# A third PSUM bank for attention, taken from the first products, with a new listed order

## The chip, the cores and the metric

The kernel runs on one core of a Trainium2 chip. Its engines work side by side: TensorE (PE) multiplies matrices and writes into PSUM, which has eight banks of 128 partitions x 512 float32 here; VectorE (DVE) and ScalarE (ACT) read PSUM, compute and write SBUF; GpSimd (POOL) issues a few transfers; the queue of SyncE (SP) issues nearly all loads and stores. The metric is the device time of one execution in microseconds (us).

## The reference

A linear attention with a decaying state is followed by two feed-forward layers with 3072 tokens, 384 features and 2048 hidden features.

```python
# attention: 4 x 8 heads, 768 steps, 48 features
state = alpha[:, :, t, :, None] * state + einsum('bhd,bhe->bhde', k[:, :, t], v[:, :, t])
y[:, :, t] = einsum('bhd,bhde->bhe', q[:, :, t], state)
...
# layer 0
h = x @ w_in                       # 3072 x 384 by 384 x 2048
g = where(h >= 1, h, where(h <= -1, 0, (h + 1) ** 2 / 4))
x = g @ w_out                      # 3072 x 2048 by 2048 x 384
...
# layer 1, with its own weights
h = x @ w_in
g = h * clip(h + 3, 0, 6) / 6
out = g @ w_out
```

## The kernel before

**Attention** is cut into 24 units: 12 groups of 256 tokens, each with two halves of the heads. The groups' pieces of 64 tokens are done as matrix products. A unit u goes through these steps, named here by the words that the kernel's list uses: loads by SP's queue (`L`, `Lp`, `Lk`, `Lq`, `V`); running products and scalings on VectorE (`p`, `r`, `s`, `k`, `R`; L380 to L409); transposition of the keys `T` (TensorE, L425) and its copy `kt` (ScalarE, L430); scores `S` (TensorE, L442) and their mask `m` (VectorE, L452); states of the pieces `ST` (TensorE, L468), their sums `h` (VectorE, L480 and L484) and copies `st` (ScalarE, L491); outputs `O` (TensorE, L515), copied out by `xc` (ScalarE, L541) and `xl` (VectorE, L546). Each of `T`, `S`, `ST` and `O` takes one PSUM bank of the pool `ps_a` (`ps_att`), in turn, and the bank is free when the engine behind it (`kt`, `m`, `h`, `xc` or `xl`) has read it.

**The layers** work on blocks of 512 tokens, six a layer, and on 16 steps of 128 hidden features a block. A step f has a first product `A` of nine matmuls of 128x512 into a bank of the pool `ps_h` (`ph`, L121), a gate, and a second product `B` of nine matmuls (L162) that add up in the three banks of `ps_o`. In layer 0 the gate is three steps of ScalarE (L141, L142, L143) and one of VectorE (L151), which frees the bank `ph`; then ScalarE (L154) and VectorE (L791) split the result in a high and a low part for `B`. In layer 1 the gate is one step of ScalarE (L146) and L153, L154, L791. The eight first steps of block 0 (phase 0) take plain float32 operands instead (L129 for `A`, L135 for `B`, six passes each). An `A` takes the next bank of `ps_h`, so with three banks the `A` of step f waits for the gate of step f - 3.

**Weights** come in 768 KB tiles, one a step (`LW`, L305), and are converted before use: L79 (ScalarE, `ca`), L85, L90, L96 (VectorE, `cb`, `cc`, `cd`), then a high part L113 (ScalarE) and a low part L114 (VectorE); in the list the high and low parts are `hi` (L708) and `lo` (L712). Layer 0's weights are converted in the first 100 us or so, layer 1's while the last block of layer 0 and the first of layer 1 run, from 480 us; their loads go through a ring of two buffers (`qkv_sb`). The input of a block of layer 1 is split by L168 (ScalarE) and L169 (VectorE).

**What sets the order.** From the start into the third phase the string `ORDER` (L39 to L64) gives the order: a word is a step with its unit or weight number (`A0_4` is the first product of phase 0, step 4), and `in_order` ties each instruction to the one before it on its engine. `Wn` (L339) are n filler matmuls into a bank of `ps_h` that compute nothing and keep TensorE busy while it would wait. Phases that follow are written as a loop, and the framework sets each engine's order there from the dependences and from when tiles of its pools come free; the numbers of banks go into that order.

Of the kernel before, what the change touches and what calls it, by code (L numbers as in the profile page):

```python
# [44 lines left out]
g0_1 V6 mx0_0 LW6 p8 B0_0 ca7 mx0_1 g0_2 r8 LW10 cb3 cc3 B0_1 ca6 mx0_2 LW9 cd3 hi2 k5 hi3 A0_3 z3 R5 gd3
LW8 cc4 Rc5 cd4 ca9 B0_2 Lp7 Lk7 cc5 g0_3 cd5 R6 Lq7 T5 ca8 mx0_3 S5 kt5 r6 p7 Rc6 A0_4 ca10 R7 r7 Rc7 s7
ST5 g0_4 k7 A0_5 h5 mx0_4 gd5 m5 st5 B0_3 s6 g0_5 s8 S7 k8 O5 m7 B0_4 V7 xc5 R8 L9 xl5 Rc8 k6 mv4 cb7 T6 cc7
S6 kt6 cd7 ST6 m6 A0_7 h6 cb6 st6 cc6 T7 cd6 O6 kt7 z6 lo3 gd6 ST7 V8 lo1 xc6 LW14 A0_6 h7 hi7 xl6 st7 lo7
LW13 hi5 O7 z7 mx0_5 gd7 p9 T8 V9 B0_5 xc7 R9 LW11 kt8 xl7 g0_6 lo2 mv6 ST8 lo5 LW12 g0_7 mx0_6 S8 h8 B0_6
m8 st8 Rc9 z8 mx0_7 gd8 lo0 O8 hi6 r9 B0_7 s9 L10 hi4 ca13 k9 ca11 lo4 A1_0 oc0 lo6 V10 cb9 LW15 cb10 A1_1  # L50
g1_0 cc10 p10 A1_2 g1_1 mx1_0 cb8 cb15 A1_3 gh1_0 mx1_1 ca15 gl1_0 cc15 g1_2 A1_4 cd15 cc8 gh1_1 T9 ca12
mx1_2 B1_0 gl1_1 kt9 gh1_2 cd8 g1_3 B1_1 gl1_2 cb12 cc12 g1_4 A1_5 mx1_3 cc9 hi8 mx1_4 A1_6 gh1_4 lo8 gh1_3
gl1_4 ca14 B1_2 gl1_3 g1_6 cd9 B1_3 r10 s10 hi9 g1_5 mx1_6 B1_4 k10 lo9 gh1_6 A1_7 mx1_5 xc8 gl1_6 gh1_5
cd10 A1_8 gl1_5 hi10 xl8 g1_7 lo10 S9 cb13 ST9 g1_8 m9 B1_5 h9 mx1_7 st9 cd12 A1_10 gh1_7 z9 gl1_7 gd9 mx1_8
# [842 lines left out]
```

## Time and profile before

| | us |
|---|---|
| median of 3 runs | 934.08 (934.04 to 934.58) |
| the profiled execution | 933.03 |
| its span in the trace | 931.1 |
| TensorE busy | 912.6 (98%) |
| VectorE busy | 530.9 (57%) |
| ScalarE busy | 531.2 (57%) |
| granted TensorE clock, mean | 0.996 |

The span runs from the first to the last instruction of the trace. Busy times are totals; filler matmuls count as busy. The views used below are the timeline (one row for a run of like instructions: its start, its length, what it writes and reads, and in brackets the idle time of its engine before it with the event that ended it), the list of waits, the table by stretch, and the groups of instructions by line. In a timeline row "issue" as a releaser means that the profile shows no wait.

### The profile page before, as it was taken

What the parts mean: (1) busy time and instruction counts of PE and PEld (TensorE: products, weight loads), DVE (VectorE), ACT (ScalarE), POOL (GpSimd) and SP (SyncE); (2) the same over time, 40 slices, a digit from 0 to 9 for tenths busy, and PEclk for the clock granted to TensorE, in tenths of its full rate; (3) what the DMA queues carried; (4) which work ended last, traced back from release to release, by engine and by line L of the source; (5) the groups of instructions that cost most, each with busy time, mean ns of one, the idle gap of its engine ahead of it and who ended that gap; (6) DMA issues with size and microseconds to landing.
All of it is one profiled execution on the core that took longest, in us unless ns stands there. A gap on an engine that the chain in (4) does not pass through costs nothing.

```text
span 931.1 us, 14299 instructions
## 1 busy us (share of the span) xinstructions
PE 912.6 (98%) x5800; PEld 726.3 (78%) x5805; DVE 530.9 (57%) x856; ACT 531.2 (57%) x855; POOL 40.3 (4%) x88
## 2 busy tenths in 40 slices
PE   7899999999999999999999999999999999999996
PEld 4646688888887888888888788888888888888885
DVE  8889989745665656565448985333433433333332
ACT  3786986785667666776777864433433433333332
POOL 1201101010100100000000000000000000000000
PEclk9999999999999999999999999999999999999999
DMA  8983602121223222221024430000000000000001
GB/s 313 331 306 109 231 2 77 63 73 40 98 72 125 83 72 72 69 86 57 6 69 137 135 136 1 34 1 0 34 1 1 34 0 1 34 1 1 34 1 38
DMA packets 18892, 69.34 MB, mean 74 GB/s; under 512 B 3457, under 2 KB 3777, under 8 KB 16513
## 3 DMA queue, kind: packets, MB, share of 16 engines
q1 hardware_dynamic: 16224, 66.07, 20.3%
q0 software_dynamic: 2304, 2.17, 1.1%
q8 instruction: 48, 0.79, 0.4%
q14 instruction: 28, 0.22, 0.1%
q10 hardware_dynamic: 288, 0.10, 0.1%
HBM read 61.44 MB, written 4.72 MB: 71 GB/s over the span
## 4 chain that ended last, share of the span: by engine, by line
PE 89%; DMA 5%; DVE 4%; ACT 1%; issue 1%; SPq 0%; DVEq 0%; ACTq 0%
PE po L162 39%; PE ph L121 38%; PE ps_att L515 2%; PE ps_att L468 2%; DMA qkv_sb<-in_wgt 2%; PE ps_att L442 2%; PE po L135 2%; PE ph L129 2%; DMA x<-in_wgt 1%; DMA qkv_sb<-in_qkv 1%; PE ps_att L425 1%; DVE w L114 0%; DVE qkv_sb L90 0%; DVE qkv_sb L380 0%; DVE qkv_sb L394 0%
## 5 line engine op out<-in xcount | busy, mean ns | idle before, releaser
L162 PE MATMUL po<-g,w 128*128 128x512 f32 x1656 | 410.9, 392 | 0.0
L121 PE MATMUL ph<-x,w 128*128 128x512 f32 x1512 | 370.6, 390 | 0.4 <-DVE t L151 0.4
L162 PEld LDWEIGHTS po<-g,w 128*128 128x128 f32 x1656 | 308.2, 188 | 64.8
L121 PEld LDWEIGHTS ph<-x,w 128*128 128x128 f32 x1512 | 282.9, 188 | 60.7 <-DVE t L151 1.2
L791 DVE TENSOR_TENSOR g<-t,g 128x512 fp32r<-128x512 f32 x160 | 110.5, 690 | 101.8 <-ACT g L154 101.6
L154 ACT ACTIVATE g<-t 128x512 fp32r<-128x512 f32 x160 | 100.9, 632 | 107.5 <-DVE t L153 63.2
L153 DVE SCALAR_TENSOR_TENSOR t<-t,ph 128x512 f32<-128x512 f32 x96 | 66.0, 688 | 157.5 <-ACT t L146 157.5
L146 ACT ACTIVATE t<-ph,half 128x512 f32<-128x512 f32 x96 | 66.0, 688 | 156.8 <-PE ph L121 155.1
L141 ACT ACTIVATE t<-ph,half 128x512 f32<-128x512 f32 x96 | 65.6, 684 | 38.6 <-PE ph L121 35.7
L151 DVE TENSOR_TENSOR t<-t,ph 128x512 f32<-128x512 f32 x64 | 43.6, 681 | 44.3 <-ACT t L143 44.0
L143 ACT ACTIVATE t<-t 128x512 f32<-128x512 f32 x96 | 60.7, 632 | 2.7
L142 ACT ACTIVATE t<-t 128x512 f32<-128x512 f32 x96 | 60.6, 631 | 2.4
L121 PE MATMUL ph<-turns,w 128*128 128x512 f32 x144 | 36.9, 396 | 0.0
L556 POOL DMA_DIRECT2D x<-stage x48 | 24.4, 514 | 263.8 <-DVE x L546 77.5
L380 DVE TENSOR_TENSOR_SCAN qkv_sb<-qkv_sb,zero 128x256 f32<-128x256 f32 x40 | 25.4, 676 | 12.1 <-DMA qkv_sb<-in_qkv 12.1
L121 PEld LDWEIGHTS ph<-turns,w 128*128 128x128 f32 x144 | 26.8, 188 | 6.1
L452 DVE TENSOR_TENSOR R<-ps_att,mask 64x512 int32<-64x512 int32 x40 | 27.5, 689 | 5.2 <-PE ps_att L442 4.5
L491 ACT ACTIVATE st<-sh 64x384 f32<-64x384 f32 x48 | 25.0, 521 | 9.6 <-DVE sh L484 8.4
L394 DVE TENSOR_TENSOR_SCAN qkv_sb<-qkv_sb,recs,zero 128x256 f32<-128x256 f32 x40 | 27.8, 737 | 0.6
L515 PEld LDWEIGHTS ps_att<-R,st 128*64 128x64 f32 x640 | 20.8, 138 | 9.2 <-issue 4.2
L468 PEld LDWEIGHTS ps_att<-qkv_sb,kt 64*64 64x64 f32 (+1 forms) x576 | 20.2, 135 | 7.7 <-issue 3.2
L515 PE MATMUL ps_att<-R,st 128*64 128x64 f32 x640 | 23.6, 225 | 2.4 <-DVE sh L480 1.8
(108 smaller groups left out, 656.7 us busy)
## 6 DMA issues: line engine op xcount, KB each, us to landing
qkv_sb<-in_qkv SPq DMA_DIRECT2D x18, 1216.0 KB, 5.5
qkv_sb<-in_wgt SPq DMA_DIRECT2D x16, 768.0 KB, 4.2
w<-in_wgt SPq DMA_DIRECT2D x10, 768.0 KB, 7.1
st<-in_vst SPq DMA_DIRECT2D x48, 128.0 KB, 3.1
x<-in_wgt SPq DMA_DIRECT2D x4, 768.0 KB, 12.2
out<-x SPq DMA_DIRECT2D x12, 256.0 KB, 2.2
w<-in_qkv SPq DMA_DIRECT2D x4, 512.0 KB, 7.9
w<-in_qkv SPq DMA_DIRECT2D x4, 448.0 KB, 5.3
```

The costliest lines, as they stand in the source:

```text
L121: nc.tensor.matmul(ph, w[:, a, 0, j * P:(j + 1) * P], x[:, b, j], start=(i == 0), stop=(i == 3 * KD - 1))
L141: nc.scalar.activation(t, ph, AF.Relu, scale=-0.5, bias=half)
L142: nc.scalar.activation(t, t, AF.Relu, scale=-1.0, bias=1.0)
L143: nc.scalar.activation(t, t, AF.Square)
L146: nc.scalar.activation(t, ph, AF.Relu, scale=1.0 / 6.0, bias=half)
L151: nc.vector.tensor_tensor(out=t, in0=t, in1=ph, op=ALU.max)
L153: nc.vector.scalar_tensor_tensor(out=t, in0=t, scalar=1.0, in1=ph, op0=ALU.min, op1=ALU.mult)
L154: nc.scalar.activation(g[:, 0], t, AF.Copy)
L162: nc.tensor.matmul(po[m], w[:, a, 1, m * P:(m + 1) * P], g[:, b], start=(first and i == 0), stop=(last and i == 2))
L468: nc.tensor.matmul(ps[C * h:C * h + C, c, r, :], n["kt"][k0:P, 2 * r + 1 - c // 2, C * h:C * h + C], n["v"][k0:P, 1 - c // 2, 2 * r + h, : ...
L515: nc.tensor.matmul(ps[C * h:C * h + C, r, cs], s[:, h, r, c, :], R[:, h, r, cs], start=True, stop=True)
L791: nc.vector.tensor_tensor(out=g[:, 1], in0=tt, in1=g[:, 0].bitcast(F32), op=ALU.subtract)
```

## The change

The pool of attention banks gets three instead of two, the pool of first products two instead of three. The string `ORDER` is written anew for that: the same steps in another order, and fillers of 38 matmuls in eight words instead of 35 in eight (beside the 24 before it).

```diff
-    ps_a = ctx.enter_context(tc.tile_pool(name="ps_a", bufs=2, space=PSUM))
-    ps_h = ctx.enter_context(tc.tile_pool(name="ps_h", bufs=3, space=PSUM))
+    ps_a = ctx.enter_context(tc.tile_pool(name="ps_a", bufs=3, space=PSUM))
+    ps_h = ctx.enter_context(tc.tile_pool(name="ps_h", bufs=2, space=PSUM))
...
-T1 W6 kt1 R2 V1 h0 Rc2 V0 r2 S1 LW1 s2 ST1 m1 st0 W1 LW2 h1 O0 k2 st1 p3 T2 V2 xc0 LW0 kt2 R3 O1 r3 ca2 s3
...
+Lp2 Lk2 m0 T1 S1 kt1 z0 p3 gd0 O0 Lq3 m1 ST1 xc0 V2 p2 W13 LW0 r2 h1 LW1 s2 st1 O1 k2 ca0 r3 LW3 T2 s3 xc1
```

What moves at three places follows, before and after, without the fillers where "..." stands.

On TensorE, at the start of the attention. L425 is a transposition, L442 scores, L468 states, L515 outputs; `ps_att_...` is the bank's tile, `st0` and `st1` are the states of units 0 and 1. Before:

```order
L425 MATMUL ps_att_159<-cst_sb_89,qkv_sb_137 128x128 x4
L442 MATMUL ps_att_173<-R_157,qkv_sb_137 64x64 x16
L468 MATMUL ps_att_192<-qkv_sb_137,kt_171 64x48 x16
...
L425 MATMUL ps_att_225<-cst_sb_89,qkv_sb_140 128x128 x4
...
L442 MATMUL ps_att_252<-R_190,qkv_sb_140 64x64 x16
L468 MATMUL ps_att_273<-qkv_sb_140,kt_237 64x48 x16
...
L339 MATMUL ph_294<-filler_90 128x512
L515 MATMUL ps_att_302<-R_157,st0_127 64x64 x16
L425 MATMUL ps_att_324<-cst_sb_89,w15_144 128x128 x4
L515 MATMUL ps_att_340<-R_190,st1_128 64x64 x16
```

After:

```order
L425 MATMUL ps_att_157<-cst_sb_89,qkv_sb_137 128x128 x4
...
L468 MATMUL ps_att_176<-qkv_sb_137,kt_167 64x48 x16
L442 MATMUL ps_att_200<-R_173,qkv_sb_137 64x64 x16
...
L425 MATMUL ps_att_233<-cst_sb_89,qkv_sb_140 128x128 x4
L442 MATMUL ps_att_238<-R_162,qkv_sb_140 64x64 x16
L515 MATMUL ps_att_261<-R_173,st0_127 64x64 x16
L468 MATMUL ps_att_281<-qkv_sb_140,kt_255 64x48 x16
...
L339 MATMUL ph_305<-filler_90 128x512
...
L515 MATMUL ps_att_333<-R_162,st1_128 64x64 x16
L425 MATMUL ps_att_356<-cst_sb_89,w15_154 128x128 x4
```

The outputs of unit 0 now stand right behind the scores of unit 1 and ahead of its states; the states of unit 0 stand ahead of its scores.

On TensorE, in the last block of layer 0, where layer 1's weights are converted (from about 508 us in the trace). `w12` is the weight of step 12, `ph_...` the bank's tile of its first product, `po0` the first bank of the second products, each of which has nine rows of which the first stands here. Before:

```order
L121 MATMUL ph_4842<-x_3756,w12_1620 128x512 x9
L162 MATMUL po0_4530<-g_4767,w9_1363 128x512
...
L121 MATMUL ph_4878<-x_3756,w13_1647 128x512 x9
L162 MATMUL po0_4530<-g_4794,w10_1413 128x512
...
L121 MATMUL ph_4905<-x_3756,w14_1669 128x512 x9
L162 MATMUL po0_4530<-g_4830,w11_1588 128x512
...
L121 MATMUL ph_4941<-x_3756,w15_1721 128x512 x9
L162 MATMUL po0_4530<-g_4866,w12_1620 128x512
```

After:

```order
L121 MATMUL ph_4845<-x_3759,w12_1504 128x512 x9
L162 MATMUL po0_4533<-g_4797,w10_1308 128x512
...
L121 MATMUL ph_4881<-x_3759,w13_1547 128x512 x9
L162 MATMUL po0_4533<-g_4833,w11_1326 128x512
...
L121 MATMUL ph_4908<-x_3759,w14_1579 128x512 x9
L162 MATMUL po0_4533<-g_4869,w12_1504 128x512
...
L121 MATMUL ph_4944<-x_3759,w15_1654 128x512 x9
L162 MATMUL po0_4533<-g_4896,w13_1547 128x512
```

Each first product now has the second product of a step one later ahead of it: that of step 14 stands behind the second product of step 11 instead of step 10.

On ScalarE, at the end of the same block. `t_4924` and `t_4927` belong to the gate of step 14, `t_4960` and `t_4963` to step 15, `g_4929` and `g_4932` are the high part of step 14's result. Before:

```order
L142 ACTIVATE t_4924<-t_4924 128x512
L143 ACTIVATE t_4924<-t_4924 128x512
L168 ACTIVATE x_5266<-x1_94 128x1536
L113 ACTIVATE w9_5022<-qkv_sb_4922 128x768
L141 ACTIVATE t_4960<-ph_4941,half_92 128x512
L154 ACTIVATE g_4929<-t_4924 128x512
L79 ACTIVATE qkv_sb_4958<-qkv_sb_4958 128x768
```

After:

```order
L142 ACTIVATE t_4927<-t_4927 128x512
L113 ACTIVATE w9_5025<-qkv_sb_4925 128x768
L154 ACTIVATE g_4896<-t_4891 128x512
L143 ACTIVATE t_4927<-t_4927 128x512
L79 ACTIVATE qkv_sb_4961<-qkv_sb_4961 128x768
L141 ACTIVATE t_4963<-ph_4944,half_92 128x512
L168 ACTIVATE x_5269<-x1_94 128x1536
L154 ACTIVATE g_4932<-t_4927 128x512
```

The split L168, which stood right behind step 14's gate, now stands behind a conversion (L79) and the first gate step of step 15; the high part of step 14 stands behind it as before.

Elsewhere in the loop's phases first and second products alternate in both kernels.

## Rows read from the trace of the kernel before

**Rows 1.** Page, part 1: engine, busy us (share of the span), instructions
```profile
PE 912.6 (98%) x5800; PEld 726.3 (78%) x5805; DVE 530.9 (57%) x856; ACT 531.2 (57%) x855; POOL 40.3 (4%) x88
```

**Rows 2.** List of waits of TensorE, 60 to 925 us: total, times, longest (us)
```profile
PE ph L129 <- DVE w L96: 1.3, 1, 1.3
PE ph L121 <- DVE t L151: 0.4, 1, 0.4
```

**Rows 3.** Table by stretch: length, busy us by engine, PEclk, DMA share, GB/s
```profile
10.00:60.00 50.00, 42.09 (x551) 27.69 (x554) 43.93 (x85) 34.49 (x57) 6.51 (x13) 0.97 0.97 338
30.00:40.00 10.00, 8.81 (x142) 6.99 (x143) 9.53 (x18) 7.20 (x15) 2.52 (x6) 0.83 0.90 317
480.00:560.00 80.00, 79.61 (x350) 65.27 (x349) 68.11 (x94) 61.96 (x93) 0.00 (x0) 1.00 0.41 138
```

**Rows 4.** Timeline of TensorE, 8 to 31 us: start, length, ..., idle before
```profile
14.55 0.63 PE L425 MATMUL ps_att<-cst_sb,qkv_sb 128*128 128x128 f32 x4 [0.52 <-issue]
15.02 1.46 PE L339 MATMUL ph<-filler 128*128 128x512 bf16 x6
...
20.38 1.24 PE L515 MATMUL ps_att<-R,st 128*64 128x64 f32 x32 [1.77 <-DVE sh L480]
...
22.71 1.31 PE L515 MATMUL ps_att<-R,st 128*64 128x64 f32 x32 [0.50 <-issue]
...
30.72 0.49 PE L468 MATMUL ps_att<-w,kt 64*64 64x48 f32 x10 [2.21 <-ACT kt L430]
```

**Rows 5.** Timeline of VectorE, 12 to 36 us
```profile
18.74 1.39 DVE L452 TENSOR_TENSOR R<-ps_att,mask 64x512 int32<-64x512 int32 x2
...
29.23 1.39 DVE L452 TENSOR_TENSOR w<-ps_att,mask 64x512 int32<-64x512 int32 x2
```

**Rows 6.** Timeline of TensorE, 30 to 70 us
```profile
33.39 3.28 PE L515 MATMUL ps_att<-w,st 128*64 128x64 f32 x64
...
45.59 8.19 PE L129 MATMUL ph<-xf,w 128*128 128x512 f32 x18
...
67.18 2.85 PE L129 MATMUL ph<-xf,w 128*128 128x512 f32 x6
```

**Rows 7.** Timeline of ScalarE, 40 to 58 us
```profile
45.14 0.94 ACT L79 ACTIVATE w<-w 128x768 f32<-128x768 f32 x1 [1.85 <-DMA w<-in_wgt]
...
55.82 0.96 ACT L79 ACTIVATE x<-x 128x768 f32<-128x768 f32 x1 [1.51 <-DMA x<-in_wgt]
```

**Rows 8.** Timeline of TensorE near 292 us
```profile
292.81 2.25 PE L121 MATMUL ph<-turns,w 128*128 128x512 f32 x9
```

**Rows 9.** Timeline of VectorE near 292 us
```profile
291.92 0.68 DVE L151 TENSOR_TENSOR t<-t,ph 128x512 f32<-128x512 f32 x1
```

**Rows 10.** Timeline of TensorE, 500 to 530 us
```profile
516.81 2.20 PE L121 MATMUL ph<-x,w 128*128 128x512 f32 x9
518.85 2.20 PE L162 MATMUL po<-g,w 128*128 128x512 f32 x9
521.44 2.34 PE L121 MATMUL ph<-x,w 128*128 128x512 f32 x9 [0.40 <-DVE t L151]
```

**Rows 11.** Timeline of VectorE, 505 to 532 us
```profile
520.71 0.68 DVE L151 TENSOR_TENSOR t<-t,ph 128x512 f32<-128x512 f32 x1
...
527.92 1.76 DVE L169 TENSOR_TENSOR x<-x,x 128x1536 fp32r<-128x1536 f32 x1 [0.19 <-ACT x L168]
```

**Rows 12.** Timeline of ScalarE, 505 to 532 us
```profile
526.41 1.48 ACT L168 ACTIVATE x<-x 128x1536 fp32r<-128x1536 f32 x1
...
529.92 0.93 ACT L79 ACTIVATE qkv_sb<-qkv_sb 128x768 f32<-128x768 f32 x1
```

**Rows 13.** Groups of instructions, 480 to 560 us: busy, mean ns, idle before
```profile
L79 ACT ACTIVATE qkv_sb<-qkv_sb 128x768 f32<-128x768 f32 x14 | 13.2, 941 | 8.2 <-DMA qkv_sb<-in_wgt 8.0
...
L141 ACT ACTIVATE t<-ph,half 128x512 f32<-128x512 f32 x12 | 8.2, 683 | 0.0
...
L143 ACT ACTIVATE t<-t 128x512 f32<-128x512 f32 x12 | 7.6, 632 | 0.2
```

More of the change, by code (lines that the diff above doesn't have):

```diff
@@ L45 @@
[L45 to L54, printed above, removed]
@@ L60 @@
[L60 to L63 removed]
+Lp0 Lk0 Lp1 p0 Lq1 r0 s0 Lk1 Lq0 k0 p1 Lq2 T0 R1 W2 kt0 r1 V0 R0 Rc1 ST0 Lp3 Lk3 s1 Rc0 S0 h0 W2 V1 k1 st0
+Lp2 Lk2 m0 T1 S1 kt1 z0 p3 gd0 O0 Lq3 m1 ST1 xc0 V2 p2 W13 LW0 r2 h1 LW1 s2 st1 O1 k2 ca0 r3 LW3 T2 s3 xc1
@@ new lines @@
+W2 kt2 mv0 k3 ca1 ST2 V3 R2 cb0 T3 L4 Rc2 h2 S2 kt3 z1 R3 st2 ST3 m2 Rc3 gd1 S3 z2 LW2 h3 gd2 O2 m3 W3 st3
+V4 p4 L5 xc2 O3 r4 ca2 s4 W6 xc3 k4 ca3 mv2 R4 T4 LW4 cb3 W2 kt4 cc0 Rc4 ST4 cd0 Lp6 Lk6 S4 h4 hi0 p5 W8 gd4
+LW6 m4 st4 ca4 R5 O4 cb1 V5 Rc5 cc1 A0_0 xc4 V6 cd1 sxh LW5 xl4 ca6 A0_1 r5 s5 Lq6 g0_0 k5 LW7 cb5 S5 g0_1
+mx0_0 cc3 B0_0 L8 cd3 ca5 mx0_1 ca7 cc5 B0_1 hi3 cb2 cc2 hi1 LW8 cd2 T5 m5 A0_2 kt5 LW10 hi2 cb4 z3 p6 gd3
+ST5 LW9 r6 g0_2 s6 A0_3 Lp7 Lk7 h5 ca8 mx0_2 gd5 k6 B0_2 cd5 Lq7 st5 cc4 g0_3 cd4 T6 p7 A0_4 kt6 ca9 R7
@@ new lines @@
+mx0_3 Rc7 r7 ST6 g0_4 s7 O5 k7 ca10 h6 B0_3 V7 mx0_4 st6 L9 cb7 xc5 z6 cc7 A0_5 xl5 R6 mv4 lo1 gd6 S7 lo0
+g0_5 cd7 T7 B0_4 m7 kt7 Rc6 mx0_5 hi4 cb6 ST7 cc6 hi5 cd6 S6 h7 A0_6 m6 st7 z7 lo5 gd7 O7 lo4 g0_6 B0_5 lo2
+V9 LW11 p8 xc7 hi6 xl7 O6 r8 LW12 mx0_6 A0_7 xc6 R8 xl6 ca11 V8 lo3 mv6 Rc8 LW14 B0_6 s8 g0_7 k8 LW13 hi7
+mx0_7 T8 lo6 ca12 B0_7 lo7 kt8 LW15 ca14 cb10 cc10 ST8 oc0 cb8 cc8 A1_0 h8 ca13 p9 st8 A1_1 cd8 g1_0 cb12
+cb9 S8 g1_1 mx1_0 A1_2 m8 gh1_0 mx1_1 hi8 O8 gl1_0 gh1_1 lo8 B1_0 g1_2 V10 gl1_1 cb13 cc12 A1_3 ca15 mx1_2
@@ new lines @@
+cb11 gh1_2 cc11 A1_4 g1_3 gl1_2 cd11 B1_1 g1_4 mx1_3 cd10 B1_2 z8 gh1_3 mx1_4 gl1_3 gh1_4 hi10 gl1_4 A1_5 r9
+gd8 cb14 cc14 hi11 L10 B1_3 cd14 g1_5 lo11 B1_4 lo10 mx1_5 cc9 gh1_5 A1_7 cd9 gl1_5 hi9 A1_6 s9 g1_7 lo9
+B1_5 g1_6 k9 mx1_7 cc13 T9 gh1_7 A1_9 cd13 kt9 xc8 gl1_7 mx1_6 ST9 g1_9 cb15 p10 A1_8 gh1_6 mx1_9 gl1_6
+A1_11 r10 g1_8 cd12 R10 B1_6 Rc10 mx1_8 s10 gh1_8 hi12 B1_7 gl1_8 gh1_9 cc15 B1_8 gl1_9 lo12 g1_11 cd15
+A1_10 R9 hi13 mx1_11 Rc9 B1_9 lo13 g1_10 sxl A1_13 gh1_11 mx1_10 hi14 gl1_11 gh1_10 A1_12 k10 g1_13 gl1_10
@@ L64 @@
+xl11 L13 mv10 B2_10 g2_12 B2_11 gh2_13 mx2_12 gl2_13 gh2_12 g2_15 gl2_12 A2_14 mx2_15 B2_12 g2_14 gh2_15
+mx2_14 gl2_15 gh2_14 gl2_14 B2_13
 """
```

18 lines of the change are left out of this document (5 added, 13 removed).

## The prediction

> **What bounds the kernel now.** The page's line on busy time comes first: TensorE works through 912.6 of 931.1 us [rows 1], so only its idle 18.5 us can be won, unless work leaves it, and none does. The list of its waits after 60 us has two entries, 1.3 and 0.40 us [rows 2]; nearly all idle time lies ahead of 60 us, where 7.91 of 50 us are idle between 10 and 60 us although the fillers there count as busy [rows 3]. In that stretch VectorE works 43.93 of 50 us and the DMA engines have a share of 0.97 [rows 3]: three resources close to full, so a wait taken from TensorE soon ends at another's.
>
> Next I read TensorE's timeline of the first 31 us [rows 4] beside VectorE's [rows 5]. With two attention banks a group of attention must wait until the group two before it has been read. The outputs of unit 0 (O0) start at 20.38, just behind the mask of unit 1 (m1, to 20.13); the states of unit 3 (ST3) at 30.72, just behind m2 (to 30.62), after 2.21 us of idle time; the transposition of unit 1 (T1, 14.55) and the outputs of unit 1 (O1, 22.71) stand in the same way behind a group of unit 0. The label on each idle time names another releaser or none, since that one was done earlier or nothing else shows: I read these as bank waits.
>
> The third place is 480 to 560 us, where layer 1's weights are converted. TensorE has 79.61 of 80 us [rows 3], but VectorE 68.11 and ScalarE 61.96, and here a gate ends late. At 521.44 the first product of step 15 waits 0.40 us for a gate's L151 [rows 2, 10]. There is one L151 a step in VectorE's queue; counted along it, the one that ends at 521.39 [rows 11] is that of step 12, the product three before, whose bank step 15 takes. With three banks the lateness of these gates costs 0.40 us in the whole kernel.
>
> **The change, front: three attention banks.** The idle times that the bank waits end are 0.52, 1.77, 0.50 and 2.21 us [rows 4], 5.0 in sum: a ceiling for what the third bank alone can give. I walked through the new list engine by engine, each group at the duration of its row and each start at the latest of its queue, its data and its bank. T1 starts at 13.8 (was 14.55), O0 at 15.6 (was 20.38, it now stands right behind the scores of unit 1 and has a bank of its own), O1 at 21.2 (was 22.71). From there VectorE sets the pace, and the lead settles: the outputs of units 2 and 3 end at 33.65 (was 36.67), the first product of the first phase starts at 42.6 (was 45.59), a lead of 3.0 us; the fifth starts at 64.35 (was 67.18) [rows 6]. Ahead of that fifth product the new list has also put 1.5 us more of TensorE work (42.4 instead of 40.9 us of products and attention groups, fillers left out, each at its row's duration), so the lead there is 2.8 + 1.5 = 4.3 us. In this walk weights land when they are asked for. With the landings of the kernel before (the conversion L79 waited 1.85 and 1.51 us for weights [rows 7]) two or three places slip, together 0.9 us: 3.4 us. The transfers ahead of that product are the same in both lists. Part of the lead is a stretch at half clock: the window 30 to 40 us has a granted clock of 0.83, which is a share of its time at 1.2 instead of 2.4 GHz, behind the idle 2.21 us [rows 3, 4]; 64 output matmuls took 3.28 us there against 1.24 for 32 elsewhere [rows 4, 6], 0.8 us too long. Without the idle time I count them at the short duration.
>
> **Front: two banks for first products.** In the listed phases a first product may start only when the gate of the product two before it has ended. The list was laid out for it: mostly over 4 us of TensorE's work lie between, against 2.9 us for the gate chain (L141 0.68, L142 and L143 0.63 each [rows 13], L151 0.68 [rows 11], hand-overs 0.3). At three places there are only 3.2; I take 0.5 us for all of them, between nothing and 1.0 (three slips of the 0.3 us by which one late conversion overruns the slack). The fillers are 38 matmuls instead of 35. Thirteen of them stand where O1 waits (13 x 1.46 / 6 = 3.2 us [rows 4], in a gap of about 4 us between the states of unit 1 and O1), so they cost nothing; if O1 were ready at once they would cost these 3.2 us.
>
> So the front gives 3.4 - 0.5 = **2.9 us**. Ends: at most 4.3, without slips. At least 0.5: if the DMA engines alone pace the front, the lead is no more than what they had idle, 0.03 x 50 = 1.5 us [rows 3], less 1.0 for the tight places.
>
> **After the listed phases: two banks.** Where layer 0 runs without conversion, the tightest place between 205 and 460 us is the first product at 292.81, whose predecessor but one had its gate end at 292.60 [rows 8, 9]: 0.2 us in time already under two banks. Elsewhere there, and in layer 1 after the conversion, where ScalarE has one step to the gate instead of three, the gate ends earlier still. I cost these stretches at nothing: the alternation of first and second products covers the gate. Where that cover is gone a step loses what the gate is late.
>
> Between 480 and 545 us it isn't covered. In the new order step 14's first product stands behind the second product of step 11, so that its turn comes at 518.85 instead of 516.81 [rows 10]; its bank is that of step 12, whose gate ends at 521.39 [rows 11]. If no gate moves, the wait is 521.39 - 518.85 = 2.54 us; the 0.40 of before goes: **2.1 us** net, the lower bound. But the queues of the gates are made anew too. Walking ScalarE's and VectorE's new order with these rows' durations, seven waits come out: 0.24, 1.6, 0.32, 0.48, 0.34, 2.05 and 0.3 us, in sum 5.3, net 4.9. The largest: the split of the next block's input (L168, 1.48 us, then L169, 1.76) stands in the old order at 526.41, ahead of the conversion L79 of 529.92 [rows 11, 12]; in the new one that L79, which needs its weights landed, and a gate step L141 stand ahead of it. Queued behind L168 is the L154 of step 14, behind it that step's L791, and the second product of step 14 waits for that. The fourteen L79 of this stretch wait 8.0 us for landings [rows 13], so late weights are the rule there. The 2.54 of the bound is in it, spread over earlier steps, which delays the later ones. The four waits below 0.35 us are within the error of such a walk; I count half of them: 5.3 - 0.6 - 0.4 = **4.3 us**, nearer to the walk than to the lower bound since the walk goes by the changed order. The upper end is 4.9.
>
> Before the change the trace shows four gaps behind masks in the front [rows 4, 5] and one of 0.40 us behind a gate after 60 us [rows 2]. The Trainium skill ("Perfetto Trace Analysis", Optimization Strategy) says that a gap which repeats on the engine that should be saturated can mean too few buffers for the next tile. By that rule alone the front lacks a bank and the stretch at 520 us, with its single gap, does not, and the time would be that of the second rival below. The trace agrees for the front; for the tail the row of the gate speaks against it, because a third bank that is just enough leaves no gap to be counted.
>
> **Sum.** The profiled execution took 933.03 us, 1.05 under the median of 934.08. 933.03 - 2.9 + 4.3 = 934.4; with 1.05 that is **935.5 us**, 0.15% more than before. About 0.2% (1.9 us, so 932.2 to 935.95) is what a measurement of this kernel can tell from no change.
>
> **Rivals.** First, slower: the weights pace the front. Point of decision: the fifth and seventh weight tiles landing later than the walk asks, so that the conversion's wait (1.51 us at 55.82 [rows 7]) comes back in full on the path of the fourth and fifth first product. The lead is then 0.5, and the time 934.08 - 0.5 + 4.3 = 937.9. For it: the share of 0.97 [rows 3]. Against it: the same tiles are asked for no later than before.
>
> Second, faster: the gates keep up. If a late second product lets the gates of steps 11 to 13 catch up, because TensorE's own waiting gives ScalarE and VectorE time, the first stall is the only one and the later ones shrink; taken to its end, two banks cost nothing beyond the 0.40 of before, and the lead stands: 934.08 - 2.9 = 931.2. For it: the engines are not full (68 and 62 of 80 us [rows 3]). Against it: the gate of step 12 is late by itself, 2.54 us, whatever TensorE does.
>
> Third, the change doesn't do what it says in the listed phases: the tight places of two banks slip by a whole gate chain (2.9 us) twice. Then the lead is 3.4 - 5.8 = -2.4, and the time 934.08 + 2.4 + 4.3 = 940.8. For it: VectorE works 43.93 of 50 us before 60 us [rows 3], so a gate easily stands behind something. Against it: the list keeps most of these places wide.
>
> **How the numbers follow.** The forecast's case has 0.57 (its own range 932.8 to 936.6: a lead of 3.4 against 2.1, a lead of 2.4 against 4.9), of which 0.40 lies within 0.2% and 0.17 above. The slower rival has 0.20 (0.17 slower, 0.03 same), the faster 0.15 (0.13 faster, 0.02 same), the third 0.08 (0.07 slower, 0.01 same). Faster 0.13, same 0.46, slower 0.41. The range reaches from 932.0, which leaves out most of the faster rival, to 938.5, which takes in the slower one and leaves out the third.
>
> **What would show it.** Right: in the profile after, T1, O0 and ST3 no longer start just behind a mask of two groups before, the first L129 group starts near 42.6 us, and the list of TensorE's waits after 60 us has L121 or L162 behind L151 and L791 with 4 to 5 us in sum, between 480 and 545 us. Wrong: if that list stays under 1 us the tail's term falls; if the L129 groups wait for L96 or the L79 at 45 to 60 us wait over 4 us in sum, weights pace the front; if L121 waits for L151 between 100 and 200 us, it is the third rival.

## The result and the profile after

The changed kernel takes 944.57 us, the median of 4 executions (942.29 to 948.63), beside 934.33 for the kernel before (934.04 to 935.55): a ratio of 1.0116, with a 95% interval of 1.0095 to 1.0137. It is slower by 1.2%. The prediction said 935.5 us, 932.0 to 938.5, with 0.46 for no change and 0.41 for slower. The likeliest case was wrong, and the time lies above the range.

The profiled execution of after took 942.29 us, with a span of 940.3 (before: 933.03 and 931.1), so the trace has to account for 9.2 us. TensorE's busy time rose from 912.6 [rows 1] to 918.4 us, which leaves 21.9 us idle instead of 18.5. Page, part 1 of after:

```profile
PE 918.4 (98%) x5808; PEld 726.4 (77%) x5808; DVE 532.1 (57%) x856; ACT 532.9 (57%) x855; POOL 39.9 (4%) x88
```

The three lists of TensorE's waits, of 0 to 60, 60 to 200 and 480 to 565 us, columns as in [rows 2]; from 200 to 480 us the list is empty:

```profile
PE ps_att L468 <- ACT kt L430: 2.0, 3, 1.2
PE ps_att L425 <- issue: 1.5, 2, 1.3
PE ph L129 <- DMA xf<-stage: 1.5, 1, 1.5
...
PE ph L121 <- DMA x<-stage: 1.0, 1, 1.0
PE po L135 <- DVE g L684: 0.6, 1, 0.6
...
PE ph L121 <- DVE t L151: 4.0, 4, 1.4
PE po L162 <- DVE g L791: 0.6, 1, 0.6
```

The waits of attention that the prediction read as bank waits are gone from this list. The 1.3 us without a releaser is unit 4's transposition at 36.04; it stands right behind the scaling of that unit's keys (L401, which ends at 35.93), so it waits for data. New in the list are waits for transfers (`xf<-stage`, `x<-stage`) and, at the end, 4.6 us behind gates where the kernel before had 0.40 [rows 2].

To see where time is lost for good, I add up the attention groups and the products in the order in which TensorE did them, without fillers and each at its line's usual length, and compare the times at which two kernels had done equal amounts. The difference, after minus before, is called the lag here (negative: ahead). It is worked out, not printed by the profile, and its size hangs on the lengths taken, so it is good to about half a microsecond:

| before's time, us | 34 | 45 | 66 | 105 | 274 to 484 | 526 | from 534 |
|---|---|---|---|---|---|---|---|
| lag of after, us | -3.7 | -2.4 | -0.8 | +1.2 | +2.3 | +5.1 | +9.2 |

Two things went wrong, of different size: the front gained its 3.7 us and then lost 6, and the stretch of the weight conversion lost 6.9.

**The front.** TensorE's timeline of after, 8 to 70 us, columns as in [rows 4, 6]:

```profile
13.93 0.63 PE L425 MATMUL ps_att<-cst_sb,qkv_sb 128*128 128x128 f32 x4 [0.25 <-issue]
...
15.56 1.18 PE L515 MATMUL ps_att<-R,st 128*64 128x64 f32 x32
...
20.91 0.33 PE L515 MATMUL ps_att<-R,st 128*64 128x64 f32 x2
...
31.95 1.41 PE L515 MATMUL ps_att<-w,st 128*64 128x64 f32 x32
...
36.04 0.63 PE L425 MATMUL ps_att<-cst_sb,qkv_sb 128*128 128x128 f32 x4 [1.28 <-issue]
...
44.76 5.45 PE L129 MATMUL ph<-xf,w 128*128 128x512 f32 x12 [1.50 <-DMA xf<-stage]
...
67.74 2.85 PE L129 MATMUL ph<-xf,w 128*128 128x512 f32 x6
```

T1, O0 and O1 start within 0.3 us of the prediction's walk (13.8, 15.6, 21.2), and the outputs of unit 3 end at 33.36 (walk: 33.65). Then it parts from the walk: the first product starts at 44.76 (walk: 42.6) and the fifth at 67.74 (walk: 64.35). The other engines' rows say what held it. ScalarE, GpSimd and VectorE of after, 20 to 53 us, then the table by stretch, columns as in [rows 3]:

```profile
34.23 0.38 ACT L541 ACTIVATE stage<-ps_att 128x256 f32<-128x256 f32 x1 [2.08 <-DMA xf<-stage]
...
46.70 0.38 ACT L541 ACTIVATE stage<-ps_att 128x256 fp32r<-128x256 f32 x1 [3.26 <-DMA xf<-stage]
...
24.59 2.71 POOL L556 DMA_DIRECT2D xf<-stage  x5 [6.20 <-ACT xf L541]
...
36.58 2.42 POOL L556 DMA_DIRECT2D xf<-stage  x5 [0.92 <-ACT xf L541]
...
35.24 0.69 DVE L401 TENSOR_TENSOR qkv_sb<-qkv_sb 128x512 f32<-128x512 f32 x1
...
10.00:60.00 50.00, 43.30 (x590) 27.81 (x589) 44.91 (x84) 34.90 (x57) 6.96 (x14) 1.00 1.00 344
```

The outputs of a group of attention go in part into one buffer, `stage`, from which six transfers of GpSimd's queue (L556, `mv` in the list) move them to the partitions where the first product wants them. The next group may write `stage` only when they have landed. Five of the six moves of the first group leave from 24.6 us on, and ScalarE waits 2.08 us for them until 34.23; five of the second leave from 36.6 us on, and both the first product (1.50 us) and ScalarE (3.26 us) wait for their landing. Both copies stand in ScalarE's queue ahead of conversions and gates. The DMA engines' share between 10 and 60 us is 1.00 (0.97 before [rows 3]). This is the account of one execution. Two others with the same list and pools, profiled below, start the first product later still, at 46.26 and 46.36 us, and there it doesn't wait for moves: unit 4's transposition waits 2.23 and 1.36 us, and the granted clock between 40 and 45 us is 0.52 and 0.50.

**The tail.** Timelines of TensorE, VectorE and ScalarE of after, 518 to 546 us:

```profile
518.04 2.20 PE L121 MATMUL ph<-x,w 128*128 128x512 f32 x9
520.08 2.20 PE L162 MATMUL po<-g,w 128*128 128x512 f32 x9
523.21 2.33 PE L121 MATMUL ph<-x,w 128*128 128x512 f32 x9 [0.93 <-DVE t L151]
525.38 2.20 PE L162 MATMUL po<-g,w 128*128 128x512 f32 x9
...
539.39 5.82 PE L121 MATMUL ph<-x,w 128*128 128x512 f32 x18 [1.37 <-DVE t L151]
...
534.17 1.76 DVE L169 TENSOR_TENSOR x<-x,x 128x1536 fp32r<-128x1536 f32 x1
...
536.31 0.69 DVE L791 TENSOR_TENSOR g<-t,g 128x512 fp32r<-128x512 f32 x1
...
538.65 0.68 DVE L151 TENSOR_TENSOR t<-t,ph 128x512 f32<-128x512 f32 x1
...
520.32 0.93 ACT L79 ACTIVATE qkv_sb<-qkv_sb 128x768 f32<-128x768 f32 x1 [2.51 <-DMA qkv_sb<-in_wgt]
521.15 0.63 ACT L142 ACTIVATE t<-t 128x512 f32<-128x512 f32 x1
```

And the table by stretch of after, columns as in [rows 3]:

```profile
480.00:560.00 80.00, 75.31 (x320) 60.31 (x319) 65.97 (x90) 60.59 (x90) 0.00 (x0) 0.98 0.41 139
535.00:540.00 5.00, 2.98 (x12) 1.80 (x11) 5.00 (x8) 3.51 (x7) 0.00 (x0) 0.91 0.24 54
540.00:545.00 5.00, 5.00 (x18) 4.02 (x17) 4.94 (x8) 3.18 (x4) 0.00 (x0) 0.75 0.34 123
```

Three things add up to the 6.9 us. First the listed waits, 4.6 us in five. Second, a wait costs more than its listed idle time: undisturbed groups start 2.04 us apart (518.04, 520.08) since the end of one overlaps the start of the next; from 520.08 to 525.38 it is 5.30 instead of 4.08, so the wait of 0.93 cost 1.22. Some 0.3 us on top of each of five waits would make 1.5. Third, after the longest wait the granted clock is below 1: the 18 matmuls of 539.39 hold TensorE until 545.04, that is 5.65 us for what takes 2 x 2.04 elsewhere, 1.6 too long. Sum 7.7, less 0.7 for the one wait that before had by the same count (0.40 and 0.3): 7.0.

### The profile page after: what moved, and what is told of

Its sections match the earlier page's. It is cut to its first block, busy times and chain, and to the rows that moved or that the text cites. A ratio compares the mean times of both kernels' runs of the same rounds, so it can differ in the third digit from the quotient of the medians.

```text
span 940.3 us, 14293 instructions
## 1 busy us (share of the span) xinstructions
PE 918.4 (98%) x5808; PEld 726.4 (77%) x5808; DVE 532.1 (57%) x856; ACT 532.9 (57%) x855; POOL 39.9 (4%) x88
## 4 chain that ended last, share of the span: by engine, by line
PE 82%; DMA 3%; DVE 2%; ACT 1%; issue 1%; ACTq 0%
PE po L162 38%; PE ph L121 38%; DMA qkv_sb<-in_wgt 3%; PE ps_att L442 2%; PE ps_att L515 2%; PE ps_att L468 2%; DVE w L114 1%; PE ps_att L425 1%; DMA x<-stage 1%; DVE qkv_sb L90 0%; DVE t L151 0%; ACT qkv_sb L79 0%; DVE x L169 0%; DVE qkv_sb L85 0%; ACT x L168 0%
## 5 line engine op out<-in xcount | busy, mean ns | idle before, releaser
L121 PE MATMUL ph<-x,w 128*128 128x512 f32 x1512 | 371.9, 392 | 5.0 <-DVE t L151 4.0
L121 PEld LDWEIGHTS ph<-x,w 128*128 128x128 f32 x1512 | 283.7, 188 | 66.2 <-DVE t L151 6.1
L791 DVE TENSOR_TENSOR g<-t,g 128x512 fp32r<-128x512 f32 x160 | 110.4, 691 | 100.4 <-ACT g L154 100.2
L141 ACT ACTIVATE t<-ph,half 128x512 f32<-128x512 f32 x96 | 65.7, 684 | 46.4 <-PE ph L121 44.7
L151 DVE TENSOR_TENSOR t<-t,ph 128x512 f32<-128x512 f32 x64 | 43.6, 681 | 40.4 <-ACT t L143 40.1
L121 PE MATMUL ph<-turns,w 128*128 128x512 f32 x144 | 36.7, 397 | 0.0
L556 POOL DMA_DIRECT2D x<-stage x48 | 24.0, 506 | 260.1 <-DVE x L546 69.3
L121 PEld LDWEIGHTS ph<-turns,w 128*128 128x128 f32 x144 | 26.9, 188 | 6.1
L468 PEld LDWEIGHTS ps_att<-qkv_sb,kt 64*64 64x64 f32 (+1 forms) x576 | 20.0, 135 | 9.5 <-issue 5.1
L515 PEld LDWEIGHTS ps_att<-R,st 128*64 128x64 f32 x640 | 20.7, 138 | 7.4 <-ACT t L142 2.8
L442 PEld LDWEIGHTS ps_att<-R,qkv_sb 64*64 64x64 f32 x640 | 20.5, 134 | 7.6 <-issue 6.1
## 6 DMA issues: line engine op xcount, KB each, us to landing
x<-in_wgt SPq DMA_DIRECT2D x4, 768.0 KB, 10.5
```

The costliest lines, as they stand in the source:

```text
L121: nc.tensor.matmul(ph, w[:, a, 0, j * P:(j + 1) * P], x[:, b, j], start=(i == 0), stop=(i == 3 * KD - 1))
L141: nc.scalar.activation(t, ph, AF.Relu, scale=-0.5, bias=half)
L151: nc.vector.tensor_tensor(out=t, in0=t, in1=ph, op=ALU.max)
L442: nc.tensor.matmul(ps[o0:o0 + C, r * NCH + c, :], n["kh"][p0:p0 + C, r, ks], R[p0:p0 + C, h, r, cs], start=True, stop=True,)
L515: nc.tensor.matmul(ps[C * h:C * h + C, r, cs], s[:, h, r, c, :], R[:, h, r, cs], start=True, stop=True)
L791: nc.vector.tensor_tensor(out=g[:, 1], in0=tt, in1=g[:, 0].bitcast(F32), op=ALU.subtract)
```

## The experiments

"Before" below is the kernel before on the same chip as the run it stands beside. Line numbers in these kernels are shifted by up to some 30 lines against the profile before; where a row has another number, the line it answers to is named.

**Which half of the change costs what.** The first kernel has the new list with its banks and gives the third bank back to first products behind the list, by a fixed turn (the last line of the diff stands where the list ends); the second is its mirror, the old list with two banks for first products behind it.

```diff
+    def bank(kind):
+        turn[kind] += 1
+        if turn["third"] == kind and turn[kind] % 3 == 0:
+            return ps_x.tile([P, NB], F32, name="third")
+        return (ps_a if kind == "att" else ps_h).tile([P, NB], F32, name="ps_att" if kind == "att" else "ph")
...
+    turn.update({"att": 0, "ph": 0, "third": "ph"})
```

> The new list with three attention banks as in the changed kernel; behind the list the eighth bank goes back to the first products, so that the loop's phases have two and three banks as before. Theory T (the third bank of first products is what the stretch 470 to 545 us lacks): that stretch loses at most 0.5 us instead of 6.9, TensorE's waits on L151 there fall from 4.0 to at most 0.5 us, the granted clock stays 1.00, and the time is 936 to 937.5 us, the front's loss of 2.3 being all that is left. Rival R (the loss there follows from the list, which hands the loop over at another time): it stays near 6 us, 943 to 945.

> The mirror image: the old list with two attention banks and three for first products; behind the list the eighth bank goes to attention, so that the loop's phases have three and two. Theory T: 934.3 + 6.9 = 941.2 us, up to 944 where the clock falls for longer; waits of TensorE on L151 and L791 of 4 to 5 us between 470 and 545 us and a granted clock under 1.00 behind the longest. Rival R: 934 to 935.

The first took 938.56 us beside 934.64 (1.0039, 1.0017 to 1.0061); between 480 and 545 us its lag grew by 0.1 us. The second took 948.68 (1.0125, 1.008 to 1.0171); there the lag grew by 5.7. TensorE's waits of the second, 300 to 600 us (L800 is L791 of before):

```profile
PE ph L121 <- DVE t L151: 3.8, 4, 1.4
PE po L162 <- DVE g L800: 0.7, 1, 0.7
```

These are much the waits of the changed kernel. So the tail's loss comes with the two banks behind the list and not with the list. Both totals lie above what was expected, by 1.1 us (937.5) and 4.7 us (944). The total of the mirror proves less: its fixed turn of banks, unlike a pool's own choice, made two first products wait 4.6 us in the middle of the old list, an artefact of my edit. The next kernel avoids that. It closes both pools where the list ends (the last two lines) and opens them again with two and three banks; it ran beside an unaltered copy of the changed kernel.

```diff
+    pools = ctx.enter_context(ExitStack())
+    open_banks(3, 2)
...
+    pools.close()
+    open_banks(2, 3)
```

> As e1_new_list_old_tail, but the banks go back by closing the two pools behind the list and opening them anew with two and three, so that the pools themselves choose the banks in the list as in the changed kernel (in e1 a fixed turn chose them). Theory T (the tail's loss is the missing third bank for first products): 470 to 545 us loses at most 0.5 us against before; the front as in the changed kernel, 1 us ahead near 60 to 95 us and 2.3 us behind from 250 us on; time 2 to 3 us over before, 936.5 to 937.5. Rival R (the hand-over from list to loop costs it): over 940.

> The changed kernel once more, beside the others on one chip. All theories: 942 to 948; the waits of TensorE after 200 us again 4.6 us in sum, between 500 and 540 us, and the granted clock under 1.00 only where a wait of over 1 us came just before, for a time that changes from one execution to the next.

Measured beside 934.91: 939.32 us (1.0043, 1.0023 to 1.0063) and 945.35 (1.0103, 1.0086 to 1.012). **By medians the new list with the bank given back costs 4.4 us, and two banks behind it another 6.0.** In its profile the copy had 4.8 + 0.5 us of waits behind L151 and L791 in the tail, and the kernel with the bank given back 0.9 + 0.3. The 4.4 is not the front alone: in that kernel's profile the lag is 5.3 us behind the front and still grows by 1.8 between 500 and 524 us, where at most 0.5 was expected, and its time is 1.8 us above the expected 937.5. In the copy the lag is 6.3 us behind the front, where the changed kernel's first profile has 2.3, and grows by 6.3 in the tail. So the tail's share repeats well, and the front's does not. In both of these profiles the front loses most at two places: about 4 us between 38 and 45 us, and another 3.5 to 4 us between 103 and 106 us, where the first product of the second phase waits 2.1 and 1.7 us for moved outputs (`x<-stage`; 1.0 in the first profile) and the granted clock is 0.66 between 105 and 110 us.

**What makes two banks cost in the tail.** The prediction put the largest stall on the split L168 and L169, which the new order sets behind a conversion. One kernel was meant to leave that split out (the second block of layer 1 takes the first block's input); another leaves out the loads and conversions of layer 1's weights (layer 1 uses those of layer 0).

```diff
+        if b == 1:
+            x_t[NBLK + 1] = x_t[NBLK]
+            return
```

> The changed kernel without one of the five splits of layer 1's inputs: block 1 takes the split input of block 0, so L168 and L169 fall away near 533 us and nothing else; the work of TensorE is the same. Theory S (the late split is the largest single stall, as the prediction has it: 2.05 us): the wait of a second product on L791 near 537 us (0.64) and that of a first product on L151 behind it (1.37) go, and with them the half clock at 540 us; 2 to 4 us under e10. Rival K (the conversion alone keeps the gates late): these waits stay within 0.7 us and the time within 0.7 us of e10.

```diff
+            if i >= NF:
+                w_t[i] = w_t[i - NF]
...
-            if last1 and f == LAG:
-                w_load(NF + 2)
-            if ((last1 and f > LAG) or (layer == 1 and bi == 0)) and t % 3 != 1 and conv_n[2] < 2 * NF:
-                w_whole(conv_n[2] + 1)
-                w_parts(conv_n[1])
-                w_load(min(conv_n[1] + 2, 2 * NF))
```

> The changed kernel without the loads and the conversion of layer 1's weights: layer 1 takes layer 0's converted weights, the work of TensorE is the same, and the split L168 and L169 stays. Theory K (the conversion keeps the gates late, and two banks cost only beside it): TensorE's waits between 470 and 545 us fall from 4.6 to at most 0.5 us, and that stretch loses at most 0.5 us against before; 6 us under e10, 938 to 940. Rival S (the alternation on two banks is too tight by itself): more than 2 us of waits stay.

The first of the two took 944.57 us beside 934.91 (1.0108, 1.0082 to 1.0134), with waits of 3.6 + 0.7 us and a lag of +5.5 in the tail. But its edit did not do what it was meant to. ScalarE, then VectorE of it:

```profile
536.59 1.50 ACT L168 ACTIVATE x<-x 128x1536 fp32r<-128x1536 f32 x1
...
538.12 1.76 DVE L169 TENSOR_TENSOR x<-x,x 128x1536 fp32r<-128x1536 f32 x1
```

A split still stands where the changed kernel has one (532.65, L169 at 534.17). The trace holds five splits instead of six, and the one that is gone is that near 601 us, where nothing waits. So this run says nothing about the split; it is one more measurement of the changed kernel's tail. Without the conversion: 938.17 beside 934.09 (1.0058, 1.0037 to 1.0078). Its table by stretch:

```profile
480.00:560.00 80.00, 80.00 (x355) 66.24 (x354) 29.14 (x42) 44.77 (x70) 0.00 (x0) 1.00 0.00 1
```

TensorE doesn't idle at all, with two banks, and the lag shrinks by 1.0 us there. So two banks cost only beside the conversion. The split by itself costs nothing: this kernel has it too, at 529.84 us. Whether it adds to the waits beside the conversion was not shown; in the changed kernel L169 (to 535.93) stands ahead of the L791 for which a second product waits 0.64 us, and that is all that can be put down to it. This kernel drops the loads and the conversion's work together; the waits of 2.51 us for a landing at 520.32 (after, above) speak for the landings, but they weren't tried apart.

**What the front would give without its new waits.** Two kernels on top of the first of all took the new waits in turn: the first two groups of attention got buffers of their own for their staged outputs; then two steps of the list were set earlier as well (`xc3` ahead of `ca2`, `S8` ahead of `A1_0`).

```diff
-            st = a1.tile([P, 2, AG], F32R if bi else F32, name="stage")
+            if g < 2:
+                st = g_p.tile([P, 2, NB], F32, name="g")[:, :, 0:AG]
+            else:
+                st = a1.tile([P, 2, AG], F32R, name="stage")
```

> As e1_new_list_old_tail, but the outputs of groups 0 and 1 are staged in buffers of their own (two of the gate's, which stand empty there) instead of the one stage buffer. Theory M (the front's lead went where the copy of unit 2's outputs waits 2.08 us for the moves of group 0 to land, and so the moves of group 1 and the first product behind them): the copy starts 2 us earlier, the first product near 43.2 us instead of 44.76, and the time is 1 to 1.6 us under e1. Rival D (the DMA engines are full, share 1.0, and deliver the moves of group 1 when they would anyway): the first product still starts after 44.3 us and the time is that of e1 within 0.4.

> As e3_own_stages, and the copy of unit 3's outputs stands ahead of the weight conversion of tile 2 on ScalarE, and the scores of unit 8 stand ahead of the first product of the second phase, which waits 0.97 us for the moves of group 3 near 103 us. Theory M: moves of group 1 another 0.9 us earlier, and 1.0 us less idle time near 103 us: 1 to 2 us under e3, 933 to 935 us in all. Rival D: only the second edit gives something, 0.5 to 1.0 us under e3.

They took 938.38 and 938.34 us beside 934.64 (1.0039, 1.0018 to 1.006; 1.0037, 1.002 to 1.0055): no gain, against the 1 us or more that moves as the only limit would have given. The wait of the first product on the moves shrank to 0.6 us, but the next limit took it over. TensorE of the first of the two, then VectorE (L695 is L684 of before):

```profile
55.12 5.49 PE L135 MATMUL po<-g,w 128*128 128x512 f32 x6 [3.33 <-DVE g L695]
...
53.91 0.56 DVE L85 TENSOR_SCALAR w<-w 128x768 int32<-128x768 int32 x1 [4.23 <-DMA w<-in_wgt]
54.38 0.68 DVE L695 TENSOR_TENSOR g<-t,ph 128x512 f32<-128x512 f32 x1
```

The gate stands right behind a conversion that waits 4.23 us for its weight. So the next kernel also changes the order of SP's loads: attention's loads of unit 6, which nobody needs yet, go behind the weight of step 7 and the first second product.

```diff
-... Rc4 ST4 cd0 Lp6 Lk6 S4 h4 hi0 p5 W8 gd4
-LW6 ... A0_0 xc4 V6 cd1 sxh LW5 xl4 ca6 A0_1 r5 s5 Lq6 g0_0 k5 LW7 cb5 S5 g0_1
+... Rc4 ST4 cd0 S4 h4 hi0 p5 W8 gd4
+LW6 ... A0_0 xc4 cd1 sxh LW5 xl4 ca6 A0_1 r5 s5 g0_0 k5 LW7 Lp6 Lk6 V6 cb5 S5 g0_1
```

> As e5_new_list_pools, with the three edits of e4_front_mended, and on SP's queue the loads that are needed late (the parts of unit 6 and its values) stand behind the weight tiles 5 to 7. Theory W (weights and moves pace the new list's front: the DMA engines are full there): the second product of step 0 starts 2 us earlier than in e4 (52 instead of 54.2), the lead over before grows to 2.5 to 3.5 us near 70 us, of which 1 is lost near 103 us; 3 us under e5, so 933 to 934.5. Rival V (VectorE's order paces it): within 0.7 us of e5.

934.25 us beside 934.91 (0.9992, 0.9979 to 1.0005), and 5.1 us less than the kernel with pools opened anew, on which it is built. It also has the buffers and the two earlier steps of the kernels above, which gave nothing there; the order of the loads alone was not tried. Its table by stretch:

```profile
10.00:60.00 50.00, 44.40 (x614) 29.11 (x617) 46.94 (x89) 37.18 (x61) 7.03 (x14) 1.00 1.01 339
```

Its TensorE waits of 60 to 200 us (L692 and L694 are L684 and L686 of before):

```profile
PE po L135 <- DVE g L692: 1.4, 1, 1.4
PE ph L121 <- DVE t L694: 0.8, 1, 0.8
```

Between 60 and 95 us its lag is -3.0: the lead that the prediction's walk had. By 106 us it is about -1.3, and from 250 us on +0.5. It is lost again in the listed phases behind the front, where the two rows stand.

**Can the lead be kept?** Three kernels followed that loss, each a step on top of the last: `ca11`, which waits for a weight, behind the gate `g0_7`; `ca0` behind copies of the first groups; the outputs and copies of unit 6 and their moves about 4 us earlier, with `ca0` and `ca1` later still.

```diff
-... O6 ... A0_7 xc6 R8 xl6 ca11 V8 lo3 mv6 ... B0_6 s8 g0_7 k8
+... O7 O6 ... xc7 xl7 xc6 xl6 mv6 ... A0_7 R8 V8 lo3 ... B0_6 s8 g0_7 ca11 k8
```

> As e6_loads_by_need, and the conversion step of weight tile 11 (which waited 2.08 us for its landing) stands behind the gate of the last step of the first phase on ScalarE instead of ahead of it. Theory W: the second product behind that gate no longer waits 1.40 us near 97 us; 1.0 to 1.6 us under e6, so about 933. Rival D: VectorE or the moves of group 3 are late next, within 0.5 us of e6.

> As e11_gate_first, and the conversion step of weight tile 0 (which waits for its landing at 22.9 us) stands behind the copies of unit 1's outputs and of unit 2's keys on ScalarE, and behind the moves of group 0. Theory W: the states of unit 2 start 0.8 us earlier and the moves of group 0 a us earlier; 0.3 to 1.0 us under e11, 932 to 933. Rival D (L4's landing at 32 us sets the pace behind it): the gain is gone by 45 us, within 0.3 us of e11.

> As e12_copies_first, with the outputs of unit 6, their copies and the moves of group 3 about 4 us earlier (ahead of the second product of step 5), and the conversion steps of tiles 0 and 1 behind the copy of unit 2's queries. Theory M (the lead of the front goes at 103 us, where the first product of the second phase waits for the moves of group 3 to land): that wait (1.30 us) falls under 0.2 and of the lead at least 1.5 us more is left at 110 us than in e12; median 932 to 933.3. Rival D (VectorE is late there anyway): the wait moves to a gate, within 0.5 us of e12.

934.79 and 934.0 us beside 934.09 (1.0003, 0.9991 to 1.0015; 0.9999, 0.9986 to 1.0011), and 934.25 beside 935.21 (0.9987, 0.9972 to 1.0001). None is beyond the noise of the one before it. In each the wait aimed at went away and another came. In the first two profiles the lead is gone by 34 us already, behind waits of 2.5 and 1.4 us for ScalarE and with a granted clock of 0.50 and 0.53 between 30 and 35 us. There the first product of the second phase waits 1.3 us for moved outputs; in the third the lead of 3.0 us lasts until 100 us, and then TensorE's waits of 60 to 200 us are one row, behind the gate of the first product two before (L694 is L686 of before):

```profile
PE ph L121 <- DVE t L694: 2.5, 1, 2.5
```

Its ScalarE, 98 to 106 us:

```profile
100.62 0.91 ACT L79 ACTIVATE w<-w 128x768 f32<-128x768 f32 x1 [2.76 <-DMA w<-in_wgt]
...
104.74 0.69 ACT L141 ACTIVATE t<-ph,half 128x512 f32<-128x512 f32 x1
```

And its table by stretch:

```profile
105.00:110.00 5.00, 2.54 (x7) 1.99 (x7) 3.16 (x5) 4.87 (x9) 0.00 (x0) 0.74 0.00 0
```

The gate's first step L141 starts at 104.74 behind two conversions and two sets of copies; the first of these conversions waits 2.76 us for its weight, and ScalarE does not idle from there on. This is what the prediction's third rival described, a tight place of two banks that slips by most of a gate chain, at one place; the lag goes from about -3 us to +1.1 at 110 us, with a granted clock of 0.74 between 105 and 110 us.

**Is it the clock?** The last kernel of this line has nine more fillers at three idle places of the front (`W2` becomes `W4`, a new `W3`, `W6` becomes `W10`).

```diff
-W2 kt2 ... Rc2 h2 S2 ... O3 r4 xc3 s4 W6
+W4 kt2 ... Rc2 h2 W3 S2 ... O3 r4 xc3 s4 W10
```

> As e13_outputs_first, with nine fillers more at three places between 23 and 38 us where TensorE otherwise waits (two ahead of the states of unit 2, three ahead of the scores of unit 2, four ahead of the transposition of unit 4). Theory C (a stretch at half clock follows an idle time of one to two microseconds in the front): the granted clock stays 1.00 up to 50 us in this profile, and the times lie closer together, 0 to 1.5 us under e13 in the median. Rival F (fillers stand in the way of attention groups): up to 1 us over e13.

934.8 us beside 935.21 (0.9992, 0.998 to 1.0005). The granted clock stays at 1.00 in every stretch up to 120 us. But up to 105 us it is 1.00 in the profile of the kernel that this one is built on, too, so in these two executions the fillers had no fall to prevent where they stand. Between 66 and 106 us TensorE is ahead by some 2 us instead of 3, and the time is the same within the noise. What the falls of the clock cost on average is left open by this run.

**The third bank without the new list.** The mirror of the question: the old list, in which attention borrows one of the second products' banks until the first second product needs it, so that first products keep their three.

```diff
-    ps_a = ctx.enter_context(tc.tile_pool(name="ps_a", bufs=2, space=PSUM))
+    ps_a = ctx.enter_context(tc.tile_pool(name="ps_a", bufs=1, space=PSUM))
...
+        free = [k for k in att["used"] if k not in att["live"] and (k < 2 or att["po"])]
+        k = min(free, key=lambda k: att["used"][k])
...
+        if k == 2:
+            return ps_o.tile([P, NB], F32, name="po2")
```

> The kernel before with its own list and its two and three banks, but until the first second product the attention may also use one bank of the second products (po2), which stands empty until then. Theory B (bank waits are what the old front loses, 5.0 us of idle time): T1, O0, O1 and ST3 start 0.5 to 2.2 us earlier and the time falls by 1 to 3 us. Rival L (in the old order other things come next: the weight step of the first tile that waits for its landing ahead of m2, and the list itself, laid out for two banks): within 0.7 us of before.

933.26 us beside 934.09 (0.9992, 0.998 to 1.0004). Its TensorE waits, 0 to 60 us (L443, L490 and L539 are L425, L468 and L515 of before):

```profile
PE ps_att L443 <- issue: 3.3, 2, 2.2
...
PE po L490 <- ACT kt L448: 1.3, 1, 1.3
PE po L539 <- DMA st<-in_vst: 1.0, 1, 1.0
```

With a bank free, the four groups that the prediction read as waiting for one start 0.5 to 1.9 us earlier (T1 14.04, O0 19.05, O1 22.23, ST3 28.82 us), so that reading holds. But the groups wait for their data instead; the two waits without a releaser end right behind the scaling of the keys (L401). The lead of 2.7 us at 32 us has turned into a lag of about 2.5 by 47 us, with a granted clock of 0.52 between 40 and 45 us, and 0.6 is left of that from 66 us on. The expected gain of 1 to 3 us is not there. The bank alone is worth at most 0.2%, even where it costs first products nothing.

## Why the prediction was wrong, step by step

- **The walk of the attention groups was right** as far as it went: T1, O0, O1 and the end of O3 came within 0.3 us. The four gaps of before were waits for banks, as the kernel with the borrowed bank showed; that of O1 is not behind a mask, as the paragraph on the Trainium skill has it, but behind the copy of unit 0's outputs, which ends at 22.62.
- **The front's term (2.9 us of gain) failed; measured, it is 2.3 us of loss in the first profiled execution, 4.4 to 6.3 in the four others of this list with these pools, and by medians 4.4 with a part of the tail in it.** The step that failed is the sentence that from O1 on VectorE sets the pace and the lead settles. The walk had the engines' instructions in it but not GpSimd's moves, nor the single `stage` buffer that ties ScalarE's queue to their landing, and it took loads to land when asked for, with 0.9 us for slips. What held the first product back differs between the executions: mostly the moves (1.50 us) in the first; in the copy and the kernel with pools opened anew unit 4's transposition (2.23 and 1.36 us), for which VectorE had waited 1.35 and 0.48 us until a load landed, and the lower clock behind it. The kernel with own buffers and loads by need has the lead of 3.0 us until 95 us, so what the walk worked out could be had. The first rival, that the weights pace the front, came nearest with a lead left of 0.5. But the sign that was named for it, over 4 us of waits of L79 between 45 and 60 us, is not there: 0 in the first profile, 1.4 us in the copy. What landed late first were moves and attention's loads; a late weight held a gate by 4.23 us only where the moves had buffers of their own. That transfers land later here since the list asks for others earlier, at a share of 1.00, is likely, and only the kernel with loads by need speaks for it.
- **The term for tight places in the listed phases (0.5 us) was too small where a lead is really there.** In the kernel that kept the lead longest, one place cost 2.5 us. In the changed kernel itself this never showed, since the moves held it first; L121 does not wait for L686 there between 100 and 200 us.
- **The tail's term (4.3 us) had the right place and cause, and measured 6.9 in the profile and 6.0 by medians.** The waits in the list are 4.6 us, between 480 and 545 us and behind L151 and L791, as the prediction asked for. Mis-sized was what a wait costs: 0.3 us more than its idle time, five times, and in the profiled execution some 1.6 us at a lower clock. The step on the largest single wait failed: the second product behind L168 and L169 waits 0.64 us and not 2.05, and the largest waits are first products' on L151 (1.37, 1.01 and 0.93 us). The run that was to show what the split costs left it in, so its part stays open. The Trainium skill ("Perfetto Trace Analysis", Optimization Strategy) says that a gap which repeats can mean too few buffers. Read in reverse, as the prediction weighed it, that gave 931.2 us; the trace disagrees with this reading, since a stretch with one gap of 0.40 us lost 6.0 when its third bank was taken.
- **Two banks cost nothing from 205 to 460 us**, as costed: the changed kernel has no wait there. The lag does rise by 1.1 us between 175 and 276 us without a wait in the list; the two kinds of work alternate in another way there, but I did not test it.
- **The sum and its range.** By medians the front came out 4.4 + 2.9 = 7.3 us and the tail 6.0 - 4.3 = 1.7 us above their terms: 935.5 + 9.0 = 944.5, the measured time. How the 9.0 divides between the two is less sure, since a part of the 4.4 lies in the tail. The range had no end in which the front loses, beside the third rival that it left out, and no bound for a lower clock behind the new waits.

## What to carry to other kernels

A buffer that is just enough leaves no gap to be seen: before taking it away, compare the end of what frees it with its next use along the whole stretch, and count for each place that then waits some 0.3 us more than the idle time. When a wait at the head of a kernel is taken away, follow every queue to the end of the stretch, that of a helper engine and the single buffer behind it too: here, with the transfers at a share of 1.00, the gain ended at the first landing that did not move. And giving a resource back when its use is over (here by closing and opening pools, worth 6.0 us) is to be weighed before a fixed split. Last, look into the trace of an experiment for the instruction that it was to remove: one edit here removed another of the same line.
